# Attention, gated layer and routed experts on one core: other places for the first loads, and another first expert step

## The chip, the cores and the metric

The program runs on one core of a Trainium2 chip. The metric is the time of one execution on the device in microseconds (us). TensorE (PE) multiplies, VectorE (DVE), ScalarE (ACT) and GpSimd (POOL) work element by element, and SyncE (SP) issues most transfers. A lower time is better.

## The reference

Three stages follow each other. All inputs are 32-bit floats.

```
# attention: 4 batches x 8 heads, 576 positions, 64 wide
scores = q @ k.T / 8 + (cum[:, None] - cum[None, :])   # cum = cumsum(log(clip(f, 1e-4, 1)))
scores = where(above the diagonal, -1e9, scores)
attn   = exp(scores - rowmax) ;  attn /= attn.sum + 1e-9 ;  x = attn @ v
# gated layer: 2304 tokens x 512, 1536 inside
x = (sigmoid(x @ w_gate) * (x @ w_val)) @ w_out
# routing to 8 experts with 288 places each: the largest logits x @ w_gate2 choose first
order = argsort(-logits.flatten())
for idx in order: give the token to the expert, if the token is free and the expert has a place
# experts, 1024 inside
out[tokens of e] = maximum(x[tokens of e] @ w1[e], 0) @ w2[e]
```

## The kernel before, in words

The order of the work is written out by hand: each engine runs its instructions in the order in which the code names them, and waits only for data and for free buffers. Transfers that SyncE issues go through one queue.

**Attention** (`attention`) goes head by head. For a pair of heads `load` brings q and k, transposed, into one of three buffers (`raw`), and `load_v` the values (`vf`). `prep` copies a head on ScalarE into `P` (`P1`, one of four buffers) in the reduced 32-bit float of TensorE, `prep2` computes the rests that this copy loses on GpSimd into `p` (`P2`), and `copies` fills the other half of `p` from `P` by two transfers. The decay enters as two rows of `P`: heads 0 and 1 get them from `ck` (`decay`), all others get them with the load, from a copy of all decay rows in device memory (`ckd`), which `decays` reads back (`raw<-ckd`) and which therefore must have landed. `ones` and the memsets in the list of `P1` set the rows of ones that belong to them.

Then `maxpass` computes the scores roughly and takes each row's maximum on VectorE, `mrows` turns the maxima into a row (`mr`), and `mstore` sends this row of 2.5 KB into row 66 of `P` (`P<-mr`). Only with it in place can `scores` run: it subtracts the maximum inside the matmul (`py`, `p1b`). ScalarE takes the exponentials (`e`), GpSimd cuts the diagonal blocks, and `av` multiplies by the values one head later. In the steady state of the loop, head h runs `scores(h)`, then `av(h-1)` with the row of maxima of head h+2 and the maxima of head h+3 between its matmuls. Heads 0 to 2 have an order of their own. `warm` gives TensorE matmuls without use while nothing else is there. From head 2 on `fill` loads the first weights of the gated layer (`mr<-ww`, two transfers of 512 KB at head 2).

**Into the first expert.** After the gated layer and the routing (`Route`), the tokens of the first expert are gathered by their indices (`First.gather`, three gathers of 96 rows on GpSimd), and one late tile of tokens is multiplied by a 0/1 matrix `hot` instead. `First.turn` turns them: for each quarter of the 512 values three matmuls by the identity and one by `hot`, then ScalarE and VectorE split the result into `xe0h` and `xe0l`. `filler` gives TensorE the last matmuls of the gated layer meanwhile. `Experts.split` splits a block of expert weights (`eraw`, or `fraw` for the first four) into `ehi` on ScalarE and `elo` on GpSimd, every fourth block after the first on VectorE. `experts` then runs per expert layer 1 (`eh`, `hh`, `hl`) and layer 2 (`ey`).

Of the kernel before, what the change touches and what calls it, by code (L numbers as in the profile page):

```python
# [34 lines left out]
def make_consts(ev, pool, keep):  # L35

    nc = ev.nc

    jp = pool.tile([128, 128], I32, name="jp")
    nc.gpsimd.iota(jp, pattern=[[1, 128]], base=0, channel_multiplier=-1)  # L40
    ev.identb = pool.tile([128, 128], BF16, name="identb")
    nc.vector.tensor_scalar(ev.identb, jp, 0.0, None, op0=OP.is_equal)
    yield
    ev.mq = pool.tile([128, S], BF16, name="mq")
    nc.vector.memset(ev.mq[:, :448], 0.0)
    nc.vector.tensor_scalar(ev.mq[:, 448:], jp, 0.0, BIG, op0=OP.is_gt, op1=OP.mult)
    ev.identr = pool.tile([128, 128], F32R, name="identr")
    nc.vector.tensor_scalar(ev.identr, jp, 0.0, None, op0=OP.is_equal)
    yield
    ev.ident = keep.tile([128, 128], F32, name="ident")  # L50
    nc.vector.tensor_scalar(ev.ident, jp, 0.0, None, op0=OP.is_equal)
    yield

AT = (2, 4)
FIRST = {2: -3, 4: -2, 5: -1}
WARM = (19, 4, 6, 2)
KT = [(0, 0, 0, 1024), (0, 128, 128, 0), (0, 256, 256, 512), (0, 384, 384, 832), (64, 448, 512, 448)]


def attention(ev, qkT, vr, f, xs, rec, ckd, fill):
# [4 lines left out]
    with ExitStack() as ctx:  # L67
# [11 lines left out]
        def load(p):  # L79
            r = RAW3[p % 3]  # L80
            nc.sync.dma_start(r[0:64], qkT[2 * p:2 * p + 2].rearrange("h d s -> d h s"))
            RAW[2 * p], RAW[2 * p + 1] = r[:, 0], r[:, 1]
# [7 lines left out]
            nc.sync.dma_start(VF[p], vr[p])  # L90

        load(0)
        load(1)
        consts = make_consts(ev, st, ev.consts)
        zero = st.tile([NHEAD, 1], F32, name="zero")
        idle = st.tile([NHEAD, 1], F32, name="warm")
# [1 line left out]
        nc.scalar.activation(idle, zero, AF.Ln, bias=1.0)  # L98
        next(consts)
        P1 = [st.tile([67, 64 + 2 * S], F32R, name=f"P1_{i}") for i in range(4)]  # L100
        for t in P1:
            nc.gpsimd.memset(t[64:67].bitcast(F32), 1.0)
            nc.gpsimd.memset(t[0:64, 0:64].bitcast(F32), 0.0)

        junk = st.tile([128, 1600], BF16, name="mj")
        JT = (0, 64, 256, 576, 1024)
        ck = st.tile([NHEAD, 2, S], F32R, name="ck")
        next(consts)
        nc.vector.tensor_scalar(ft, ft, 1e-4, 1.0, op0=OP.max, op1=OP.min)
        nc.scalar.activation(ft, ft, AF.Ln)  # L110
        cum = st.tile([NHEAD, S], F32, name="cum")
        nc.vector.tensor_tensor_scan(cum, ft, zero.to_broadcast([NHEAD, S]), 0.0, op0=OP.add, op1=OP.add)
        nc.vector.tensor_scalar(ck[:, 0], cum, -8.0, None, op0=OP.mult)
        nc.vector.scalar_tensor_tensor(ck[:, 1], cum, -8.0, ck[:, 0], op0=OP.mult, op1=OP.subtract)

        def ones(p):
            nc.gpsimd.memset(RAW3[p][64:66, :, :S], 1.0)
# [9 lines left out]
        def decay(h):  # L127
            nc.sync.dma_start(P1[h % 4][64:66, K0:].bitcast(F32), ck[h:h + 1].bitcast(F32))
# [46 lines left out]
        def maxpass(h):  # L175
            for _ in maxparts(h):
                pass
# [7 lines left out]
        def mstore(h):  # L185
            nc.sync.dma_start(P1[h % 4][66:67, 0:640].bitcast(F32), MR.pop(h))
# [73 lines left out]
        warm(WARM[0])  # L260
        for h in (0, 1):
            decay(h)
        nc.sync.dma_start(ckd.rearrange("r h s -> h r s"), ck.bitcast(F32))
        for h in (0, 1):
            prep(h, 64)
# [21 lines left out]
        load_v(0)  # L287
        copies(2)
        decays(2)
        load(2)  # L290
        copies(3)
        warm(WARM[3])
        maxpass(2)
# [1 line left out]
        ones(2)  # L295
        for h in range(1, NHEAD):
            odd = h % 2
            scores(h, 3 if h == 2 else None)
            if h == 1:
                ones(0)  # L300
            if h == 2:
                mstore(3)
                next(consts)

            def rows(r):
                if r < NHEAD:
                    mrows(r)
                    mstore(r)

            def early():  # L310
                rows(h + 2 if h > 1 else 2)
                if h == 1:
                    prep(4)
                    prep2(4)
                elif h + 4 < NHEAD:
                    prep(h + 4)

            def late():
                if h + 3 < NHEAD:
                    maxpass(h + 3)  # L320

            if h == 1:
                av(0, {2: early, 3: lambda: maxpass(3)})
                prep(5)
            elif h == 2:
                av(1, {0: lambda: maxpass(4), 5: early})
                late()
            else:
                av(h - 1, {AT[0]: early, AT[1]: late})
            if h < NHEAD - 3:  # L330
                copies(h + 3)
            if h >= 3 and odd:
                store(h // 2 - 1)
            if h == 1:
                load(3)
                decays(3)
            if not odd and h // 2 + 3 < NPAIR:
                load(h // 2 + 3)
                decays(h // 2 + 3)
            if odd and h // 2 + 1 < NPAIR:  # L340
                load_v(h // 2 + 1)
            for b in range(B - 1):
                step = {2: 0, 4: 1, 5: 2}.get(h - (b + 1) * H)
                if step is not None:
                    recip(b, step)
            if h + 4 < NHEAD:
                prep2(h + 4)
            if h in FIRST:
                fill(FIRST[h])
            fill(h)  # L350
# [596 lines left out]
class Experts:  # L947
# [24 lines left out]
    def split(self, n, part=None, after=None):  # L972

        if part is not None:
            nc, c = self.ev.nc, slice(512 * part, 512 * part + 512)
            if part == 0:
                self.hi[n] = self.first.tile([128, 1024], F32R, name=f"ehi{n % 12}", bufs=1)
                self.lo[n] = self.first.tile([128, 1024], F32R, name=f"elo{n % 12}", bufs=1)
                nc.scalar.activation(self.hi[n], self.raw[n], AF.Copy)
            nc.gpsimd.tensor_copy(self.gate, after)  # L980
            nc.gpsimd.tensor_tensor(self.lo[n][:, c], self.raw[n][:, c], self.hi[n][:, c], op=OP.subtract)
            if part:
                del self.raw[n]
                if n < 3:
                    self.load(n + 1)
        elif n < 8 * E:
            nc, r = self.ev.nc, self.raw.pop(n)
            pool = self.first if n % 12 < 4 else self.pool
            hi = self.hi[n] = pool.tile([128, 1024], F32R, name=f"ehi{n % 12}", bufs=1)
            lo = self.lo[n] = pool.tile([128, 1024], F32R, name=f"elo{n % 12}", bufs=1)  # L990
            nc.scalar.activation(hi, r, AF.Copy)  # L991
            eng = nc.vector if n % 4 == 3 and n > 3 else nc.gpsimd
            eng.tensor_tensor(lo, r, hi, op=OP.subtract)  # L993
            self.load(n + RAWS)

# [5 lines left out]
class First:  # L1001
# [7 lines left out]
        self.xg = [t[:TT] for t in (slots[:, :DM], slots[:, DM:], big)]  # L1009
        self.x = [pool.tile([128, 4, CH], F32R, name=n) for n in ("xe0h", "xe0l")]  # L1010

    def gather(self, route):
        nc = self.nc
        for i in range(3):
            nc.gpsimd.indirect_dma_start(out=self.xg[i], out_offset=None, in_=self.x2d,  # L1015
                                         in_offset=bass.IndirectOffsetOnAxis(ap=self.ev.idx[:, i:i + 1], axis=0))
        places = self.places[:, :CH].bitcast(I32)
        nc.gpsimd.iota(places, pattern=[[1, CH]], base=0, channel_multiplier=0)
        nc.vector.tensor_scalar(self.hot[:, :CH], places, route.slot[:, LAST:LAST + 1], None, op0=OP.is_equal)  # L1019

    def turn(self, x, bank):

        nc = self.nc
        for k in range(4):
            ks = slice(k * 128, (k + 1) * 128)
            p = bank()
            for i in range(3):
                nc.tensor.matmul(p[:, i * TT:(i + 1) * TT], self.xg[i][:, ks], self.ev.ident[:TT, :TT], start=i == 0,  # L1028
                                 stop=False, skip_group_check=True)
            nc.tensor.matmul(p[:, :CH], x[:, ks], self.hot[:, :CH], start=False, stop=True, skip_group_check=True)  # L1030
            nc.scalar.activation(self.x[0][:, k], p[:, :CH], AF.Copy)
            nc.vector.tensor_tensor(self.x[1][:, k], p[:, :CH], self.x[0][:, k], op=OP.subtract)


def experts(ev, W, x2d, first, idx, out, wk, psum):
# [108 lines left out]
def network(tc, qk, vv, f, ww, bcT, w1, w2, cb, cf, out):  # L1144
# [3 lines left out]
    with ExitStack() as ctx:  # L1148
# [86 lines left out]
            R.round(r == 0, FILL[5] if r < ROUNDS - 1 else 6, lambda: r and EW.split((r - 1) // 2, (r - 1) % 2, R.c[:1, 0, :1, 0]))  # L1235
        a = R.settle()
        R.permutation(a)
        filler(left - 2 * 3 * NF)
        X0 = First(ev, ep, scratch, x2d)
        X0.gather(R)  # L1240
        for part in range(2):
            EW.split(3, part, ev.idx[:1, :1])
        filler(left)
        next(rest, 0)
        X0.turn(xd, F.bank)
# [2 lines left out]
        ps.close()  # L1248
        EW.pool = pool("ew")
        xw = pool("xw", bufs=2)  # L1250
        pools = {n: pool("xp_" + n, bufs=b, space=PSUM) for n, b in (("h", 3), ("y", 2), ("t", 3))}
        experts(ev, EW, x2d, X0.x, ev.idx, out, xw, lambda n: pools[n].tile([128, 512], F32, name="e" + n))


# [28 lines left out]
```

## Time and profile before

| | |
|---|---|
| median of 3 runs | 921.29 us (920.33 to 921.76) |
| the profiled execution | 920.34 us, span 918.4 us |
| TensorE busy | 899.2 us (98%) |
| VectorE, ScalarE, GpSimd busy | 549.5, 330.2, 461.4 us |
| moved by transfers | 111.30 MB, mean 121 GB/s |

Times in the profile count from the span's start. A busy TensorE is not a fast one: the granted clock says how much of its full speed it had. An engine's idle time is put down to what ended last before the waiting instruction started.

### The profile page before, as it was taken

How to read it: one execution, taken by the hardware profiler on the slowest of the kernel's cores; microseconds unless marked ns; L12 is line 12 of the kernel's file. 1: busy time of each engine (PE TensorE's matmuls, PEld its weight loads, DVE VectorE, ACT ScalarE, POOL GpSimd, SP SyncE). 2: the span in 40 equal slices, each digit the busy share in tenths (PEclk: the TensorE clock that was granted, in tenths of full speed). 3: DMA queues.
4: the chain of work that ended last, by engine and by line, in shares of the span. 5: the costliest groups of instructions: out<-in, count | busy, mean ns of one | idle time of the engine just before them, and what ended most of it. 6: DMA issues, size and time to landing. Idle time of an engine off the chain costs nothing. (4 is left out here: it accounts for less than half of the span.)

```text
span 918.4 us, 14090 instructions
## 1 busy us (share of the span) xinstructions
PE 899.2 (98%) x5206; PEld 753.1 (82%) x5206; DVE 549.5 (60%) x1183; ACT 330.2 (36%) x570; POOL 461.4 (50%) x393
## 2 busy tenths in 40 slices
PE   8899999999999999999999999999999999999995
PEld 5677777778788888888888887887788999999995
DVE  5387887918885497988989642525523443444431
ACT  5566677642323111121111221221125444444530
POOL 8678899825555122121222221321158777777741
PEclk9899999999999999999999999999999999999998
DMA  6788899745652203010121210011257666657610
GB/s 141 169 209 224 228 233 251 205 121 184 164 163 64 75 1 92 18 67 9 46 63 26 67 46 1 1 44 46 71 166 228 195 189 194 199 169 210 206 32 26
DMA packets 49016, 111.30 MB, mean 121 GB/s; under 512 B 11346, under 2 KB 11762, under 8 KB 48946
## 3 DMA queue, kind: packets, MB, share of 16 engines
q1 hardware_dynamic: 44786, 98.85, 38.6%
q0 software_dynamic: 3072, 9.44, 3.2%
q10 hardware_dynamic: 1088, 2.10, 0.7%
q8 instruction: 41, 0.67, 0.3%
q14 instruction: 29, 0.24, 0.1%
HBM read 86.12 MB, written 14.71 MB: 110 GB/s over the span
## 5 line engine op out<-in xcount | busy, mean ns | idle before, releaser
L509 POOL TENSOR_TENSOR gl<-sg,gh 128x512 fp32r<-128x512 f32 x36 | 49.5, 1375 | 201.0 <-ACT gh L508 201.0
L993 POOL TENSOR_TENSOR elo<-eraw,ehi 128x1024 fp32r<-128x1024 f32 x45 | 109.0, 2431 | 43.0 <-ACT ehi L991 42.6
L141 PE MATMUL pv<-e,vf 128*65 128x256 f32 (+1 forms) x434 | 106.6, 370 | 0.0
L500 PE MATMUL gv<-xah,w_hi 128*128 128x512 f32 (+1 forms) x288 | 103.1, 358 | 0.0
L500 PE MATMUL gv<-xah,w_lo 128*128 128x512 f32 (+1 forms) x288 | 102.7, 357 | 0.0
L500 PE MATMUL gv<-xal,w_hi 128*128 128x512 f32 (+1 forms) x288 | 102.7, 357 | 0.0
L542 DVE CUSTOM_DVE_ANT_0 mb<-mb,bc 128x512 f32<-128x512 f32 x96 | 82.1, 856 | 3.3
L542 DVE CUSTOM_DVE_ANT_0 mb<-mr,bc 128x512 f32<-128x512 f32 x96 | 81.7, 851 | 2.8
L508 ACT ACTIVATE gh<-sg 128x512 fp32r<-128x512 f32 x36 | 22.8, 633 | 156.4 <-PE o L521 84.2
L1080 PE MATMUL ey<-hh,ehi 128*128 128x288 f32 x256 | 78.2, 305 | 0.0
L500 PE MATMUL gv<-xbh,w_hi 128*128 128x512 f32 x192 | 76.7, 399 | 0.0
L1080 PE MATMUL ey<-hl,ehi 128*128 128x288 f32 x256 | 76.3, 298 | 0.0
L1080 PE MATMUL ey<-hh,elo 128*128 128x288 f32 x256 | 75.9, 296 | 0.0
L500 PE MATMUL gv<-xbh,w_lo 128*128 128x512 f32 x192 | 75.9, 395 | 0.0
L500 PE MATMUL gv<-xbl,w_hi 128*128 128x512 f32 x192 | 75.8, 395 | 0.0
L141 PEld LDWEIGHTS pv<-e,vf 128*65 128x65 f32 x434 | 50.4, 139 | 24.1 <-issue 15.4
L1067 PE MATMUL eh<-xeh,ehi 128*128 128x288 f32 x224 | 68.0, 304 | 0.0
L1070 DVE SCALAR_TENSOR_TENSOR hl<-eh,hh 128x288 fp32r<-128x288 f32 x64 | 29.0, 456 | 63.8 <-ACT hh L1069 63.8
L157 DVE CUSTOM_DVE_ANT_0 mj<-p1b,mq 128x192 bf16<-128x192 f32 (+3 forms) x128 | 46.6, 418 | 34.3 <-PE p1b L141 34.2
L141 PE MATMUL p1b<-P 66*128 66x192 f32 (+7 forms) x256 | 65.9, 326 | 0.9 <-DVE mx L157 0.4
L1067 PE MATMUL eh<-xeh,elo 128*128 128x288 f32 x224 | 66.4, 297 | 0.0
L1067 PE MATMUL eh<-xel,ehi 128*128 128x288 f32 x224 | 66.4, 296 | 0.0
(214 smaller groups left out, 2304.8 us busy)
## 6 DMA issues: line engine op xcount, KB each, us to landing
eraw<-w SPq DMA_DIRECT2D x56, 512.0 KB
mr<-ww SPq DMA_DIRECT2D x26, 512.0 KB
raw<-qk SPq DMA_DIRECT2D x16, 576.0 KB
p<-P SPq DMA_DIRECT2D x64, 144.0 KB
vf<-vv SPq DMA_DIRECT2D x16, 330.0 KB
bc<-ww SPq DMA_DIRECT2D x10, 512.0 KB
xs<-xo SPq DMA_DIRECT2D x16, 292.5 KB
x2d<-mr SPq DMA_DIRECT2D x17, 256.0 KB
```

What stands on the lines that cost most here:

```text
L141: nc.tensor.matmul(out, lhsT, rhs, start=start, stop=stop, skip_group_check=True)
L157: nc.vector.tensor_tensor_reduce(out=junk[:, JT[t]:JT[t] + n], in0=src, in1=ev.mq[:, S - n:], op0=OP.add, op1=OP.min, scale=-1.0, scalar=3 ...
L500: nc.tensor.matmul(p[i][:, :m], w_[:, ws], x_[:, k], start=n == 0, stop=n == 11)
L508: nc.scalar.activation(hi, s, AF.Copy)
L509: nc.gpsimd.tensor_tensor(lo, s, hi, op=OP.subtract)
L542: nc.vector.tensor_tensor_reduce(out=junk, in0=a, in1=self.bc[j], op0=OP.mult, op1=OP.add, scale=1.0, scalar=0.0, accum_out=res)
L993: eng.tensor_tensor(lo, r, hi, op=OP.subtract)
L1067: nc.tensor.matmul(p[:, :CH], w_[:, ws], x_[:, k], start=n == 0, stop=n == 11)
L1070: nc.vector.scalar_tensor_tensor(h[1][:, f], p[:, :CH], 0.0, h[0][:, f], op0=OP.max, op1=OP.subtract)
L1080: nc.tensor.matmul(p[:, :CH], w_[:, ws], h_[:, f], start=n == 0, stop=n == 23)
```

## The change

In the first heads the loads of q and k, the rows of maxima and the copies of heads 4 and 5 change places on SyncE's queue, and the work of heads 1 to 3 is ordered anew around them. The fixed rows of `P1` are set by ScalarE and VectorE. In the step into the first expert, `hot` and the last halves of `elo` come before the gathers, the turns by the identity become transposes that all come before the products by `hot`, block 7 of the expert weights is split on GpSimd, and the PSUM pools are laid out in another order. The identity matrix is made later.

```
@@ attention @@
-WARM = (19, 4, 6, 2)
+WARM = (18, 4, 6, 2)
         load(0)
-        load(1)
...
-        for t in P1:
-            nc.gpsimd.memset(t[64:67].bitcast(F32), 1.0)
-            nc.gpsimd.memset(t[0:64, 0:64].bitcast(F32), 0.0)
...
         nc.scalar.activation(ft, ft, AF.Ln)
+        for t in P1[:2]:
+            nc.scalar.activation(t[64:67], zero[0:3].to_broadcast([3, 64 + 2 * S]), AF.Copy, bias=1.0)
...
+        for t in P1[2:]:
+            nc.vector.memset(t[64:67].bitcast(F32), 1.0)
...
         for h in (0, 1):
             decay(h)
+        load(1)
+        for t in P1:
+            nc.gpsimd.memset(t[0:64, 0:64].bitcast(F32), 0.0)
         nc.sync.dma_start(ckd.rearrange("r h s -> h r s"), ck.bitcast(F32))
...
         decays(2)
-        load(2)
         copies(3)
...
-            scores(h, 3 if h == 2 else None)
-            if h == 1:
-                ones(0)
             if h == 2:
+                mrows(3)
                 mstore(3)
-                next(consts)
+                load(3)
+                decays(3)
+                load_v(1)
+            scores(h)
...
             if h == 1:
-                av(0, {2: early, 3: lambda: maxpass(3)})
+                ones(0)
+                av(0, {2: lambda: rows(2), 3: lambda: maxpass(3)})
+                load(2)
+            elif h == 2:
+                prep(4)
+                prep2(4)
+                av(1)
                 prep(5)
-            elif h == 2:
-                av(1, {0: lambda: maxpass(4), 5: early})
+                prep2(5)
+                maxpass(4)
+            elif h == 3:
+                av(2, {2: lambda: rows(4), 3: lambda: maxpass(5), 5: lambda: prep(6)})
+                rows(5)
+                prep(7)
                 late()
+                prep2(6)
...
-            if h < NHEAD - 3:
+            if h == 2:
+                copies(4)
+                copies(5)
+            elif 2 < h < NHEAD - 3:
                 copies(h + 3)
...
-            if h == 1:
-                load(3)
-                decays(3)
+            if h == 2:
+                load_v(2)
...
-            if odd and h // 2 + 1 < NPAIR:
-                load_v(h // 2 + 1)
+            if odd and h > 1 and h // 2 + 2 < NPAIR:
+                load_v(h // 2 + 2)
...
+            if h > NHEAD - 3:
+                next(consts)
@@ Experts.split @@
-            eng = nc.vector if n % 4 == 3 and n > 3 else nc.gpsimd
+            eng = nc.vector if n % 4 == 3 and n > 7 else nc.gpsimd
@@ First @@
+    def tokens(self, route):
+        places = self.places[:, :CH].bitcast(I32)
+        nc.gpsimd.iota(places, ...)
+        nc.vector.tensor_scalar(self.hot[:, :CH], places, route.slot[:, LAST:LAST + 1], None, op0=OP.is_equal)
...
     def turn(self, x, bank):
+        for i in range(3):
+            for k in range(4):
+                nc.tensor.matmul(p[k][:, i * TT:(i + 1) * TT], self.xg[i][:, rows[k]], self.ev.ident[:TT, :TT], start=i == 0,
+                                 stop=False, is_transpose=True, skip_group_check=True)
         for k in range(4):
-            for i in range(3):
-                nc.tensor.matmul(p[:, i * TT:(i + 1) * TT], self.xg[i][:, ks], self.ev.ident[:TT, :TT], start=i == 0,
-                                 stop=False, skip_group_check=True)
...
@@ network @@
+        X0 = First(ev, ep, scratch, x2d)
+        X0.tokens(R)
+        for part in range(2):
+            EW.split(3, part, X0.hot[:1, :1])
         filler(left - 2 * 3 * NF)
-        X0.gather(R)
-        for part in range(2):
-            EW.split(3, part, ev.idx[:1, :1])
+        X0.gather()
         filler(left)
...
-        ... (("h", 3), ("y", 2), ("t", 3))}
+        ... (("t", 3), ("y", 2), ("h", 3))}
```

SyncE's queue at the program's start, before; `raw_103` takes heads 0 and 1, `raw_104` heads 2 and 3, `P_0` and `P_1` are the buffers of heads 0 and 1:

```order
L81 DMA raw_103<-qk 64x2x1152
L81 DMA raw_104<-qk 64x2x1152
L128 DMA P_0_116<-ck 2x1x576
L128 DMA P_1_117<-ck 2x1x576
L263 DMA ckd<-ck 32x2x576
L132 DMA p_165<-P_0_116 64x576
L133 DMA p_165<-P_0_116 64x576
L86 DMA raw_104<-ckd 2x2x576
L132 DMA p_167<-P_1_117 64x576
L133 DMA p_167<-P_1_117 64x576
L186 DMA P_0_116<-mr 1x5x128
```

The same place now:

```order
L82 DMA raw_103<-qk 64x2x1152
L128 DMA P_0_115<-ck 2x1x576
L128 DMA P_1_116<-ck 2x1x576
L82 DMA raw_104<-qk 64x2x1152
L266 DMA ckd<-ck 32x2x576
L132 DMA p_164<-P_0_115 64x576
L133 DMA p_164<-P_0_115 64x576
L87 DMA raw_104<-ckd 2x2x576
L132 DMA p_166<-P_1_116 64x576
L133 DMA p_166<-P_1_116 64x576
L186 DMA P_0_115<-mr 1x5x128
```

The second load of q and k has moved behind the two decay rows and stands directly ahead of the store of `ckd`.

SyncE's queue at heads 2 and 3, before, from the values of heads 2 and 3 on; `P_3`, `P_0` and `P_1` are here the buffers of heads 3, 4 and 5, `raw_104` takes heads 8 and 9, and `mr_428` and `mr_430` are the first weights of the gated layer:

```order
L90 DMA vf<-vv 128x660
L186 DMA P_3_119<-mr 1x5x128
L186 DMA P_0_116<-mr 1x5x128
L132 DMA p_341<-P_1_117 64x576
L133 DMA p_341<-P_1_117 64x576
L81 DMA raw_104<-qk 64x2x1152
L86 DMA raw_104<-ckd 2x2x576
L396 DMA mr_428<-ww 128x512
L396 DMA mr_430<-ww 128x512
L186 DMA P_1_117<-mr 1x5x128
```

The same transfers now, from the values of heads 2 and 3 on:

```order
L91 DMA vf<-vv 128x660
L132 DMA p_365<-P_0_115 64x576
L133 DMA p_365<-P_0_115 64x576
L132 DMA p_378<-P_1_116 64x576
L133 DMA p_378<-P_1_116 64x576
L91 DMA vf<-vv 128x660
L82 DMA raw_104<-qk 64x2x1152
L87 DMA raw_104<-ckd 2x2x576
L411 DMA mr_404<-ww 128x512
L411 DMA mr_406<-ww 128x512
L186 DMA P_0_115<-mr 1x5x128
L186 DMA P_1_116<-mr 1x5x128
```

The row of maxima of head 4 (`P_0<-mr`) has moved from ahead of the load and the two weight transfers to behind them; the load of heads 4 and 5 and that of heads 6 and 7, not in these rows, now stand behind the rows of heads 2 and 3.

GpSimd at the step into the first expert, before; `x2d` holds the tokens, `elo` the rests of the weights:

```order
L1015 DMA mr_5435<-x2d,idx 96x512 x2
L1015 DMA mr_5434<-x2d,idx 96x512
L1018 IOTA mb_5436 128x288
L980 CAST gate<-idx 1x1
L981 TENSOR_TENSOR elo_6132<-fraw,ehi_6131 128x512
L980 CAST gate<-idx 1x1
L981 TENSOR_TENSOR elo_6132<-fraw,ehi_6131 128x512
L1045 DMA xg<-x2d,idx 96x512 x3
```

The same place now:

```order
L1031 IOTA mb_5435 128x288
L995 COPY gate<-mb_5436 1x1
L996 TENSOR_TENSOR elo_6128<-fraw,ehi_6127 128x512
L995 COPY gate<-mb_5436 1x1
L996 TENSOR_TENSOR elo_6128<-fraw,ehi_6127 128x512
L1037 DMA mr_5434<-x2d,idx 96x512 x2
L1037 DMA mr_5433<-x2d,idx 96x512
L1065 DMA xg<-x2d,idx 96x512 x3
```

The three gathers have moved behind the two halves of `elo`, which now wait for `hot` (`mb_5436`) instead of the indices.

## Rows read from the trace of the kernel before

**Rows 1.** Page, busy times; then stretches: us, busy (instructions), clock, transfers.

```profile
PE 899.2 (98%) x5206; PEld 753.1 (82%) x5206; DVE 549.5 (60%) x1183; ACT 330.2 (36%) x570; POOL 461.4 (50%) x393
...
680.00:700.00 20.00, 16.96 (x115) 16.58 (x115) 7.46 (x11) 10.58 (x17) 14.56 (x8) 0.91 0.85 263
```

**Rows 2.** Who waited for whom, TensorE: us in total, times, longest.

```profile
PE eh L1067 <- DVE hl L1070: 2.1, 1, 2.1
PE py L141 <- DMA P<-mr: 2.0, 1, 2.0
PE eh L1067 <- DVE xe0l L1032: 1.0, 1, 1.0
...
PE p1b L141 <- ACT e L206: 0.4, 1, 0.4
```

**Rows 3.** SyncE in order of time, first heads: start, us to issue, transfer.

```profile
9.33 0.39 SPq L263 DMA_DIRECT2D ckd<-ck  x1
...
11.50 0.24 SPq L86 DMA_DIRECT2D raw<-ckd  x1
...
13.12 2.96 SPq L186 DMA_DIRECT2D P<-mr  x2
...
18.32 0.67 SPq L81 DMA_DIRECT2D raw<-qk  x1
...
21.62 0.75 SPq L186 DMA_DIRECT2D P<-mr  x1
```

**Rows 4.** TensorE in order of time: scores of heads 0, 2, 4; layer 1's first.

```profile
15.01 0.39 PE L141 MATMUL py<-P 67*128 67x256 f32 x1
...
26.11 0.38 PE L141 MATMUL py<-P 67*128 67x256 f32 x1 [2.04 <-DMA P<-mr]
...
42.13 0.52 PE L141 MATMUL py<-P 67*128 67x256 f32 x1
...
681.12 0.40 PE L1067 MATMUL eh<-xe0h,ehi 128*128 128x288 f32 x1 [0.99 <-DVE xe0l L1032]
```

**Rows 5.** Stretches: PE, PEld, DVE, ACT, POOL busy, clock, transfer share, GB/s.

```profile
37.00:53.00 16.00, 16.00 (x98) 12.31 (x97) 10.04 (x36) 10.28 (x17) 11.36 (x13) 1.00 0.90 237
27.00:33.50 6.50, 6.14 (x23) 4.16 (x22) 2.21 (x10) 2.04 (x5) 5.40 (x6) 0.65 0.87 190
...
28.90:35.70 6.80, 6.80 (x21) 4.16 (x20) 2.21 (x10) 1.20 (x4) 3.63 (x4) 0.50 0.55 127
...
694.55:697.95 3.40, 3.32 (x14) 3.31 (x15) 0.75 (x3) 1.09 (x2) 3.40 (x2) 0.50 0.91 293
```

**Rows 6.** Page, transfers: destination<-source, count, size of one.

```profile
mr<-ww SPq DMA_DIRECT2D x26, 512.0 KB
raw<-qk SPq DMA_DIRECT2D x16, 576.0 KB
p<-P SPq DMA_DIRECT2D x64, 144.0 KB
vf<-vv SPq DMA_DIRECT2D x16, 330.0 KB
```

**Rows 7.** Chain that ended last: start, us, turns, a product by hot, later transposes.

```profile
676.66 0.64 PE gv L1028 x6
677.30 0.52 PE gv L1030 x2
...
701.46 0.25 PE et L1055 x3
```

**Rows 8.** GpSimd, TensorE's weight loads and ScalarE in order of time.

```profile
671.59 0.92 POOL L1015 DMA_INDIRECT mr<-x2d,idx  x1 [0.30 <-issue]
...
672.99 1.28 POOL L981 TENSOR_TENSOR elo<-fraw,ehi 128x512 fp32r<-128x512 f32 x1
...
675.17 0.30 PEld L1028 LDWEIGHTS gv<-ident,mr 96*128 96x128 f32 x2 [0.26 <-DMA mr<-x2d,idx]
...
687.22 1.06 ACT L991 ACTIVATE ehi<-eraw 128x1024 fp32r<-128x1024 f32 x1 [1.67 <-DMA eraw<-w]
```

More of the change, by code (lines that the diff above doesn't have):

```diff
@@ L52, in make_consts @@
     yield
+    yield
 AT = (2, 4)
 FIRST = {2: -3, 4: -2, 5: -1}
-WARM = (19, 4, 6, 2)
+WARM = (18, 4, 6, 2)
 KT = [(0, 0, 0, 1024), (0, 128, 128, 0), (0, 256, 256, 512), (0, 384, 384, 832), (64, 448, 512, 448)]
@@ L310, in early @@
             def early():
-                rows(h + 2 if h > 1 else 2)
-                if h == 1:
-                    prep(4)
-                    prep2(4)
-                elif h + 4 < NHEAD:
+                rows(h + 2)
+                if h + 4 < NHEAD:
                     prep(h + 4)
@@ L333, in attention @@
                 store(h // 2 - 1)
-            if h == 1:
-                load(3)
-                decays(3)
+            if h == 2:
+                load_v(2)
             if not odd and h // 2 + 3 < NPAIR:
@@ L345, in attention @@
                     recip(b, step)
-            if h + 4 < NHEAD:
+            if 2 < h < NHEAD - 4:
                 prep2(h + 4)
+            if h > NHEAD - 3:
+                next(consts)
             if h in FIRST:
@@ L1010, in __init__, with gather @@
         self.x = [pool.tile([128, 4, CH], F32R, name=n) for n in ("xe0h", "xe0l")]
-    def gather(self, route):
+    def tokens(self, route):
+        nc = self.nc
+        places = self.places[:, :CH].bitcast(I32)
+        nc.gpsimd.iota(places, pattern=[[1, CH]], base=0, channel_multiplier=0)
+        nc.vector.tensor_scalar(self.hot[:, :CH], places, route.slot[:, LAST:LAST + 1], None, op0=OP.is_equal)
+    def gather(self):
         nc = self.nc
@@ L1016, in gather @@
                                          in_offset=bass.IndirectOffsetOnAxis(ap=self.ev.idx[:, i:i + 1], axis=0))
-        places = self.places[:, :CH].bitcast(I32)
-        nc.gpsimd.iota(places, pattern=[[1, CH]], base=0, channel_multiplier=0)
-        nc.vector.tensor_scalar(self.hot[:, :CH], places, route.slot[:, LAST:LAST + 1], None, op0=OP.is_equal)
     def turn(self, x, bank):
         nc = self.nc
-        for k in range(4):
-            ks = slice(k * 128, (k + 1) * 128)
-            p = bank()
-            for i in range(3):
-                nc.tensor.matmul(p[:, i * TT:(i + 1) * TT], self.xg[i][:, ks], self.ev.ident[:TT, :TT], start=i == 0,
-                                 stop=False, skip_group_check=True)
-            nc.tensor.matmul(p[:, :CH], x[:, ks], self.hot[:, :CH], start=False, stop=True, skip_group_check=True)
-            nc.scalar.activation(self.x[0][:, k], p[:, :CH], AF.Copy)
-            nc.vector.tensor_tensor(self.x[1][:, k], p[:, :CH], self.x[0][:, k], op=OP.subtract)
+        p = [bank() for _ in range(4)]
+        rows = [slice(k * 128, (k + 1) * 128) for k in range(4)]
+        for i in range(3):
+            for k in range(4):
+                nc.tensor.matmul(p[k][:, i * TT:(i + 1) * TT], self.xg[i][:, rows[k]], self.ev.ident[:TT, :TT], start=i == 0,
+                                 stop=False, is_transpose=True, skip_group_check=True)
+        for k in range(4):
+            nc.tensor.matmul(p[k][:, :CH], x[:, rows[k]], self.hot[:, :CH], start=False, stop=True, skip_group_check=True)
+            nc.scalar.activation(self.x[0][:, k], p[k][:, :CH], AF.Copy)
+            nc.vector.tensor_tensor(self.x[1][:, k], p[k][:, :CH], self.x[0][:, k], op=OP.subtract)
 def experts(ev, W, x2d, first, idx, out, wk, psum):
@@ L1237, in network @@
         R.permutation(a)
+        X0 = First(ev, ep, scratch, x2d)
+        X0.tokens(R)
+        for part in range(2):
+            EW.split(3, part, X0.hot[:1, :1])
         filler(left - 2 * 3 * NF)
-        X0 = First(ev, ep, scratch, x2d)
-        X0.gather(R)
-        for part in range(2):
-            EW.split(3, part, ev.idx[:1, :1])
+        X0.gather()
         filler(left)
@@ L1250, in network @@
         xw = pool("xw", bufs=2)
-        pools = {n: pool("xp_" + n, bufs=b, space=PSUM) for n, b in (("h", 3), ("y", 2), ("t", 3))}
+        pools = {n: pool("xp_" + n, bufs=b, space=PSUM) for n, b in (("t", 3), ("y", 2), ("h", 3))}
         experts(ev, EW, x2d, X0.x, ev.idx, out, xw, lambda n: pools[n].tile([128, 512], F32, name="e" + n))
```

## The prediction

> **What bounds the kernel now.** I read the busy shares first, then the stretches, then the chain of waits and the list of who waited for whom. TensorE is busy for 98% of the span, so the change can only win where TensorE stands still or runs slowly, and it can lose wherever it makes it wait [rows 1]. The stretches show two such places in the stages that the change touches: the step into the first expert, where TensorE is busy for 16.96 of 20 us at a granted clock of 0.91 [rows 1], and the first heads, where the clock is 0.50 for 6.8 us [rows 5]. The waits give them names: 2.0 us in the first heads for the row of maxima of head 2 (P<-mr) and 0.4 us for an exponential, and at the experts 1.0 us for the last xe0l and 2.1 us for an hl [rows 2].
>
> How the first wait comes about is to be seen on SyncE's queue and on TensorE [rows 3, 4]. The row of head 0 is issued at 13.12 and TensorE goes on with it at 15.01, 1.9 us later. The row of head 2 is issued at 21.62 and TensorE can use it only at 26.11, 4.5 us later. It has the same 2.5 KB. What differs is what was issued just ahead of it: a load of 576 KB at 18.32, with copies behind it. So a small transfer on this queue lands behind the bytes ahead of it. The rate at which such a mix drains is 190 GB/s in one full stretch and 237 GB/s in another [rows 5].
>
> After each of the two long waits TensorE ran at 0.50, that is at 1.2 GHz instead of 2.4: 28.90 to 35.70, and 694.55 to 697.95 [rows 5]. Half of each is lost: 3.4 and 1.7 us. Heads of full speed follow the first from 36 us on; the scores of head 4 start at 42.13 [rows 4]. From there to the end of attention TensorE has no wait of note, so a shift of that start is a shift of the end.
>
> **What goes in the first heads.** The load of heads 4 and 5 now stands behind the row of head 2. That takes away the wait of 2.0, the 0.4 behind an exponential (the maxima of head 4 are now computed after it) and the slow clock of 3.4: minus 5.8 us.
>
> **What comes, at head 0.** The load of heads 2 and 3 used to be issued right behind the first one. It now stands behind the two decay rows and ahead of the store of ckd, and the load of the ckd rows (raw<-ckd) waits for that store to land. Queued behind that waiting load on SyncE are the two copies of head 1 and then the row of head 0. Before, ckd was issued at 9.33, its reader at 11.50, the row at 13.12 [rows 3]. Now 576 KB, 0.59 MB [rows 6], drain first: 2.5 us at 237 GB/s, 3.1 at 190. Everything behind ckd's landing moves by as much, the row too, and the scores of head 0 start at about 18.0 instead of 15.01. TensorE has nothing but finished warm-up work there. I take plus 3.0, since a lone load is nearest to the lower rate; the bounds are 0.7 (the store passes the load, and only the load's own issue time of 0.67 is in the way) and 3.7 (both). Moving the ones of P1 from GpSimd to ScalarE and VectorE and dropping one warm-up matmul I cost at nothing: that work ends before the row does. Without this cover it would be some tenths of a microsecond either way.
>
> The Trainium skill ("DMA: Bandwidth & Descriptors", section "Queues, rings and completion order") says that each DMA engine takes the descriptors of a queue in ring order, but that completion is not first in, first out over a queue, so that a later small transfer on few engines can be done before an earlier one on all sixteen. By its first half the row waits as in the last paragraph, by its second it need not; the 4.5 us of head 2 side with the first half, and the second is the first rival below.
>
> **What comes, at head 4.** In before the row of head 4 was issued one head ahead of the load of heads 8 and 9 and of the two weight loads; now it stands behind them. And the queue never runs dry on the way there. The row of head 2 is issued at 21.62 plus 3.0, that is 24.6, and the next load 0.75 later at 25.4. From there to the row of head 4 stand three raw loads of 576 KB, two vf of 330, four copies of 144 and two weight loads of 512 [rows 6]: 3988 KB, 4.08 MB, which is 17.2 us at 237 GB/s and 21.5 at 190. With the 1.9 us of an unhindered row it lands at 44.5 to 48.8. TensorE, without the waits taken away, is ready for the scores of head 4 at 42.13 minus 5.8 plus 3.0, or 39.3. A wait of 5.2 to 9.5 us; I take 5.5, because the 237 are of a stretch with the same kinds (weights, loads, copies, vf) and the 190 of one with a load and little else. Its lower bound is nothing, if the row passes what is ahead. If the clock is low before, row and readiness both move and this term stays.
>
> **The clock behind both.** Two waits of 2.0 us each brought a slow stretch that cost 1.7 and 3.4 us [rows 2, 5]. The two new waits are longer, so I set 2.6 for each, 5.2 together, between 3.4 and 6.8; the lower bound is nothing.
>
> **The first expert.** Four edits. (a) The 12 turns by the identity become transposes. Three of the old ones take 0.64 us, three transposes with the same operands' size at L1055 take 0.25 [rows 7], and all of them can run before the four matmuls by hot, 0.52 each. (b) hot is made earlier, but the two halves of elo, 1.28 each, now run on GpSimd ahead of the three gathers. The third gather ended its issue at 671.59 plus 0.92, and TensorE saw it land at 675.17 [rows 8]. It can move by nothing, if the halves are done before the stores that are gathered land, or by 2.6, both halves; I take 1.6, so 676.8. Then four transposes (0.33) and four products (2.1): layer 1 starts at 679.2. (c) PSUM pools in another order: the first layer-1 matmul needs only the first quarter of x, so the 1.0 us for xe0l is gone. Layer 1 starts at 681.12 in before [rows 4], so minus 1.9, between minus 3.5 and minus 0.6. Of this 1.1 is taken back (0 to 1.9): ScalarE's second ehi waited for its weights until 687.22 [rows 8], and it issues these behind its last quarter of x, which comes earlier by less than layer 1 does. (d) The elo of the fourth weight block goes from VectorE to GpSimd. On VectorE it stood ahead of the hl that held TensorE for 2.1; on GpSimd it is late only if layer 2 asks for it sooner than it is done. That takes 2.1 away and the slow clock of 1.7. In all 1.9 minus 1.1 plus 2.1 plus 1.7: minus 4.6 us; bounds minus 7.3, and nothing (late gathers and a late elo eat all of it).
>
> **Other edits**, at nothing: ident is made at head 30, long before its first use; load_v comes earlier into a third buffer whose readers are done; both lie beside full TensorE work.
>
> **The sum.** Minus 5.8, plus 3.0, plus 5.5, plus 5.2, minus 4.6: plus 3.3 us. The profiled run of before took 920.34 (span 918.4), the median of the runs is 921.29, 0.95 above it. On the first scale that gives 923.6, on the second 924.6; I forecast 924.5.
>
> **Rivals.** First, on the other side: the small row is not held by what is ahead of it, and head 2's wait had a reason of its own. Then the 5.5 at head 4 and its clock go; the 3.0 at head 0 stay, since there SyncE itself waits for ckd. Minus 5.8, plus 3.0, plus 2.6, minus 4.6: minus 4.8, 916.5 us on the scale of the median. It decides as soon as the row of head 4 lands less than about 4 us behind its issue. For it speaks that the row has only 2.5 KB; against it the 4.5 us of head 2. Chance 0.15.
>
> Second: waits as forecast, but no slow stretch behind them. Plus 3.3 minus 5.2: minus 1.9, 919.4 us. Against it: both waits of before had one. For it: they differed twofold in length, so the clock is not a fixed price. Chance 0.17.
>
> Third: the step into the expert gives only 1 of its 4.6 us, with GpSimd late for gathers or for the extra elo: plus 6.9, 928.2 us. For it: GpSimd is the busiest of the other engines there, with 14.56 of 20 us [rows 1], and two jobs more stand in its queue. Against it: the gathers had less than 0.3 us of wait behind them [rows 8], and the work added ahead of them is small beside their landing. Chance 0.13.
>
> The forecast keeps 0.55, with a range of its own from 921.5 to 928. A measurement of this kernel tells about 0.2% from no change, 1.84 us: below 919.4 is faster, above 923.1 slower. Faster gets the first rival and half of the second, 0.24; the same gets the other half and a tenth from the forecast's lower edge, 0.18; slower the rest, 0.58. The range from 917.5 to 930 leaves out most of the first rival below and the third with slow clocks above.
>
> **What would show it.** In the trace of the changed kernel: py of head 0 waits about 3 us for P<-mr and starts near 18; py of head 2 does not wait; py of head 4 waits 4 us or more for P<-mr and starts at 45 to 50; a granted clock of 0.50 behind both. At the expert: the first eh starts 1 to 3 us earlier against its neighbours and waits for no xe0l, nothing in layer 1 waits for hl, and the clock stays at 1.00. I am wrong if py of head 4 waits under 2 us, if the clock holds, or if layer 1 of the first expert stalls.

## The result, and the profile after

The changed kernel takes 927.63 us (median of 5 runs, 925.43 to 928.14), the kernel before 920.50 (5 runs); the ratio is 1.0073, 95% interval 1.0053 to 1.0093. It is slower, as forecast, inside the range of 917.5 to 930, and 3.1 us above the forecast of 924.5. The profiled execution took 926.05 us with a span of 924.0, 5.6 us more than the span before; the terms below are told on that scale. The 1.5 us by which the median of the runs moved more are not in this trace.

The waits of TensorE now, in the form of [rows 2] (us in total, times, longest):

```profile
PE py L141 <- DMA P<-mr: 7.5, 2, 3.8
...
PE pv L141 <- DMA vf<-vv: 0.8, 1, 0.8
...
PE gv L1047 <- DMA mr<-x2d,idx: 0.7, 1, 0.7
...
PE eh L1087 <- DVE hl L1090: 0.6, 2, 0.3
```

The one long wait for a row of maxima has become two, and the waits for xe0l and the long one for hl are gone. TensorE in order of time has, against [rows 4], the scores of heads 0, 2, 4 and 5, the gated layer's first matmul and layer 1's first:

```profile
17.65 0.39 PE L141 MATMUL py<-P 67*128 67x256 f32 x1 [3.74 <-DMA P<-mr]
...
31.12 0.33 PE L141 MATMUL py<-P 67*128 67x256 f32 x1
...
49.17 0.42 PE L141 MATMUL py<-P 67*128 67x256 f32 x1 [3.76 <-DMA P<-mr]
...
57.82 0.52 PE L141 MATMUL py<-P 67*128 67x256 f32 x1
...
209.94 0.64 PE L515 MATMUL gv<-xah,w_hi 128*128 128x512 f32 x1
...
689.19 0.51 PE L1087 MATMUL eh<-xe0h,ehi 128*128 128x288 f32 x1
```

One more row of the kernel before is needed beside it, the same first matmul of the gated layer there:

```profile
199.05 0.64 PE L500 MATMUL gv<-xah,w_hi 128*128 128x512 f32 x1
```

So attention ends 10.9 us later (209.94 against 199.05). From there to layer 1 it is 479.25 us instead of 482.07, 2.8 less, and from layer 1 to the end of the span 234.8 instead of 237.3, 2.5 less. 10.9 minus 2.8 minus 2.5 is the 5.6.

SyncE's queue in order of time shows both new waits at their source; it answers to [rows 3]:

```profile
8.10 0.67 SPq L82 DMA_DIRECT2D raw<-qk  x1
8.81 0.59 SPq L266 DMA_DIRECT2D ckd<-ck  x1
...
14.13 0.24 SPq L87 DMA_DIRECT2D raw<-ckd  x1
...
15.66 2.14 SPq L186 DMA_DIRECT2D P<-mr  x2
...
28.14 0.74 SPq L186 DMA_DIRECT2D P<-mr  x1
...
39.62 0.65 SPq L82 DMA_DIRECT2D raw<-qk  x1
...
40.80 0.81 SPq L411 DMA_DIRECT2D mr<-ww  x2
41.71 3.86 SPq L186 DMA_DIRECT2D P<-mr  x2
```

The store of ckd is issued 0.5 us sooner than before, but its reader 2.6 later: 5.3 us lie between the two issues where it was 2.2. The row of head 0 follows at 15.66. The row of head 4 is issued at 41.71 and TensorE goes on at 49.17, 7.5 us later. The row of head 2, with nothing big ahead of it, is issued at 28.14, and TensorE starts these scores at 31.12 without a wait.

Behind both waits TensorE ran slowly. The stretches, with the columns of [rows 5]:

```profile
18.90:29.10 10.20, 10.20 (x39) 8.54 (x38) 2.54 (x13) 4.60 (x8) 7.77 (x9) 0.51 0.33 91
49.60:56.40 6.80, 6.80 (x23) 5.13 (x23) 0.00 (x0) 3.18 (x5) 1.34 (x3) 0.51 0.20 67
```

10.2 and 6.8 us at 1.2 GHz, half of each lost: 8.5 us together, where the prediction had 5.2.

### The profile page after: what moved, and what is told of

It is laid out like the page before. It is cut to its first block, busy times and chain, and to the rows that moved or that the text cites. A ratio compares the mean times of both kernels' runs of the same rounds, so it can differ in the third digit from the quotient of the medians.

```text
span 924.0 us, 14086 instructions
## 1 busy us (share of the span) xinstructions
PE 899.7 (97%) x5193; PEld 752.9 (81%) x5193; DVE 544.3 (59%) x1184; ACT 333.3 (36%) x572; POOL 458.2 (50%) x390
## 5 line engine op out<-in xcount | busy, mean ns | idle before, releaser
L141 PE MATMUL p1b<-P 66*128 66x192 f32 (+7 forms) x256 | 68.2, 335 | 2.4 <-DMA P<-ck 1.3
L1006 ACT ACTIVATE ehi<-eraw 128x1024 fp32r<-128x1024 f32 x60 | 63.3, 1056 | 9.9 <-DMA eraw<-w 9.8
```

The costliest lines, as they stand in the source:

```text
L141: nc.tensor.matmul(out, lhsT, rhs, start=start, stop=stop, skip_group_check=True)
```

## The experiments

Each was timed against the kernel before on the same chip, but not all on one chip, so the rows of the table are compared with each other by their ratios. Single executions of one kernel lie up to 6 us from its median, so a verdict rests on the ratio and its interval, and a place on the trace. The last column is read from the one profiled execution of each kernel.

| edit | median us | ratio to before | gated layer starts at us |
|---|---|---|---|
| the whole change | 927.63 | 1.0073 (1.0053 to 1.0093) | 209.9 |
| attention part alone | 932.09 | 1.0105 (1.0088 to 1.0122) | 212.0 |
| expert part alone | 918.18 | 0.9969 (0.9955 to 0.9984) | 203.2 |
| block 7 on GpSimd alone | 917.76 | 0.9975 (0.9953 to 0.9996) | 198.9 |
| load of heads 2, 3 back at the start | 919.67 | 0.9984 (0.9969 to 1.0000) | 206.8 |
| row of head 4 ahead of load and weights | 922.92 | 1.0010 (0.9993 to 1.0027) | 204.7 |
| both | 916.68 | 0.9954 (0.9935 to 0.9972) | 198.6 |
| warm matmuls in the waits | 919.36 | 0.9992 (0.9976 to 1.0008) | 200.9 |
| row of head 4 in ScalarE's queue | 926.83 | 1.0074 (1.0046 to 1.0102) | 209.2 |
| rows of heads 2 and 4 there | 922.69 (1 run) | | 206.8 |
| start as before, weights behind the rows | 912.92 | 0.9901 (0.9871 to 0.9930) | 201.5 |
| start as before, load between the rows | 912.61 | 0.9900 (0.9866 to 0.9934) | 198.0 |
| the same with 7 warm matmuls | 912.53 | 0.9906 (0.9887 to 0.9925) | 194.5 |

### The two parts by themselves

The first kernel has the changed attention and the old expert step, the second the other way round:

```
attention() of the changed kernel,  Experts.split, First, network as before
attention() as before,              Experts.split, First, network of the changed kernel
```

> 

> The attention part of the change alone, with the old expert step. Theory (two independent parts): the gated layer's first matmul comes 10.9 us later, as in the changed kernel, and nothing after it changes, so 920.5 plus 10.9, about 931.4 us. Rival (the expert step's gain hangs on the later start, or is none): the same 927.6 as the whole change.

> 

> The expert part of the change alone, on the old attention. Theory: attention ends as before, layer 1 of the first expert starts 2.8 us earlier and the wait of 2.05 for hl and its slow clock are gone, less what the weights take back: minus 5.3, about 915.2 us. Rival (earlier layer 1 only runs into late weights): minus 2 or less, 918.5 or above.

The attention part alone costs 1.05% (9.7 us, 8.1 to 11.2 by the interval), where 10.9 were expected, with the waits of the whole change. Its trace ends attention 2.1 us later than that of the whole change, with a wait of 1.33 us for VectorE's maxima at 177.31 and a slow stretch behind it. The expert part alone gives 0.31% (2.9 us, 1.5 to 4.1 by the interval), less than the 5.3 expected: the median lies between theory and rival, nearer to the rival's 918.5. In its trace the stages themselves gave what they gave in the whole change: 479.42 us from the gated layer to layer 1 and 235.1 from there to the end, 4.8 less than before together. But in this execution attention, whose code is that of before, ended 4.1 us later, at 203.2. Some 3.3 of them are a wait for VectorE's maxima late in attention and a clock of 0.57 for 4 us behind it:

```profile
168.38 0.47 PE L141 MATMUL p1b<-P 67*128 67x448 f32 x1 [1.94 <-DVE mx L157]
```

The kernel before waited 0.40 us there in its profiled execution. Such a wait for the maxima of a late head is in some of the traces and not in others, from none to 1.9 us, also between kernels with the same attention; what decides it is open.

### Block 7 on GpSimd alone

```
-            eng = nc.vector if n % 4 == 3 and n > 3 else nc.gpsimd
+            eng = nc.vector if n % 4 == 3 and n > 7 else nc.gpsimd
```

> 

> The kernel before with one edit: block 7 of the expert weights is split on GpSimd instead of VectorE. Theory: the wait of 2.05 us for hl at 694.6 and the slow clock behind it (1.7) go, and nothing new comes: minus 3.7, about 916.8 us. Rival (on GpSimd the elo is late for layer 2, which then waits for it): minus 1 or less, 919.5 or above.

From layer 1's first matmul to the end of the span it is 3.9 us less than before (233.4 against 237.3), no wait for hl is left and none for elo came; the medians give 0.25% (0.4 to 4.3 us). The theory held. In the whole change this edit is the same, yet the stage behind layer 1's start gained only 2.5: 1.4 us were given back. The two waits of 0.2 and 0.3 us for hl shown above are 0.6 of that; that the rest also comes of the earlier start, as the prediction argued, is likely but not shown.

### The load of heads 2 and 3 back at the start

```
         load(0)
+        load(1)
...
         for h in (0, 1):
             decay(h)
-        load(1)
```

> 

> The whole change, but with the load of heads 2 and 3 back at the program's start. Theory (the store of ckd drains behind this load, and the slow clock behind head 0 comes from the wait): the reader of ckd is issued near 11.5 again, py of head 0 starts near 15.0 without a wait of note, and the clock of 0.50 from 18.8 to 28.1 is gone: minus 2.6 minus 4.6, about 920.4 us; the wait at head 4 stays near 3.8. Rival A (the slow clock has another cause than the wait): minus 2.6, 925.0 us. Rival B (the row of head 0 is late for the new places of the ones): py of head 0 stays near 17.6, no change, 927.6.

The scores of head 0 are back at 15.00 and run on at full clock. The time fell to 919.67, near the theory's 920.4. One thing it had not: at head 4 TensorE now came sooner and waited 4.9 us instead of 3.8. Below are its scores of heads 0 and 4, SyncE's issue of the rows of heads 4 and 5, and the slow stretch, which here began while TensorE still waited:

```profile
15.00 0.39 PE L142 MATMUL py<-P 67*128 67x256 f32 x1
...
43.29 0.58 PE L142 MATMUL py<-P 67*128 67x256 f32 x1 [4.93 <-DMA P<-mr]
```

```profile
35.85 2.66 SPq L187 DMA_DIRECT2D P<-mr  x2
```

```profile
40.80:51.00 10.20, 7.71 (x26) 6.03 (x27) 0.27 (x1) 3.17 (x5) 3.19 (x5) 0.51 0.39 121
```

From the issue of the row of head 4 to its use it is 7.4 us, as in the whole change.

### The row of head 4 ahead of the load and the weights

```
-FIRST = {2: -3, 4: -2, 5: -1}
+FIRST = {4: -2, 5: -1}
...
                 rows(5)
+                load(4)
+                decays(4)
+                fill(-3)
...
-            if not odd and h // 2 + 3 < NPAIR:
+            if not odd and h > 2 and h // 2 + 3 < NPAIR:
```

> 

> The whole change, but the load of heads 8 and 9, its decay rows and the first two weight loads are issued behind the rows of heads 4 and 5. Theory (the row of head 4 drains behind those 1600 KB): the row is usable 2 to 3 us after its issue, py of head 4 waits under 1 us, the slow clock behind it is gone: minus 3.4 minus 3.4, about 921 us. Rival A (the bytes ahead of those, copies, vf and the load of heads 6 and 7, hold it as well): minus 2 or less, 925.5 or above. Rival B (the later load makes head 8 wait instead): the gain at head 4 stands in the trace, but a new wait near 65 us takes 2 us or more of it.

The wait for the row of head 4 is gone, with its slow clock. Smaller waits stand in its place: the one for the values of heads 2 and 3, 0.85 us in the whole change, is 1.56 here, although nothing ahead of their load was moved, and one for the row of head 6 is new:

```profile
40.30 1.16 PE L141 MATMUL pv<-e,vf 128*65 128x256 f32 x4 [1.56 <-DMA vf<-vv]
45.63 0.28 PE L141 MATMUL py<-P 67*128 67x256 f32 x1
50.97 0.52 PE L141 MATMUL py<-P 67*128 67x256 f32 x1
...
58.41 0.39 PE L141 MATMUL py<-P 67*128 67x256 f32 x1 [0.52 <-DMA P<-mr]
```

So what was issued ahead of the row held it, and the row of head 6, which now stands behind the moved transfers, waits a little in its turn. By the ratios the kernel gained 0.6%, some 5.8 us, and attention ends 5.3 us sooner in the trace; the theory had 6.8, and the difference is within the noise.

### Both edits together

> 

> The whole change with both edits: the load of heads 2 and 3 back at the start, and the load of heads 8 and 9 and the first weights behind the rows of heads 4 and 5. Theory (two independent waits, each with its slow clock): minus 7.3 and minus 6.8, 927.6 to about 913.5 us, 7 us under the kernel before. Rival (once TensorE is early at head 0, the transfers are what it waits for at heads 2 to 4 anyway): 917 us or above, with a wait for a row or a load in the first eight heads.

916.68, so the rival was nearer than the theory. Attention ends at 198.6, no sooner than in the kernel before (199.05); what is left of the gain is the expert part. No slow clock is in these heads, but the DMA engines stood still for 5 us while the load stood behind two rows:

```profile
35.00:40.00 5.00, 4.73 (x30) 3.47 (x28) 3.85 (x19) 3.31 (x6) 4.15 (x6) 1.00 0.02 7
```

TensorE then waited 0.8 us for the row of head 6; 1.6 us for the values of heads 2 and 3 it had lost at 33.79, ahead of the pause.

### Work without use in the two waits

```
         mstore(1)
+        warm(16)
         scores(0)
...
+            if h == 4:
+                warm(16)
             scores(h)
```

> 

> The whole change, with 16 matmuls without use (some 3.4 us at full speed) ahead of the scores of head 0 and 16 ahead of those of head 4, in the time in which TensorE waits for the rows. They change no transfer. Theory (the slow clock comes of the idle wait, and costs 4.6 and 3.4 us): py of heads 0 and 4 start within 0.5 us of where they do now relative to their rows, the clock stays at 1.00 behind both, minus 8, about 919.6 us. Rival A (the slow clock comes of the mix of work behind the waits): no gain, 927 to 928. Rival B (it comes of idle time, but the time saved is lost again to later waits for transfers): the clock stays at 1.00, but waits of some us appear behind, and under 4 us are saved.

No transfer was changed. The row of head 4 is still used only 7.1 us after its issue (37.56 and 44.65). The granted clock is 1.00 all through both places, and 8.3 us of the median are gone (927.63 to 919.36), or 0.8% by the ratios; the theory had 8.0:

```profile
18.00:29.00 11.00, 11.00 (x69) 8.70 (x68) 4.29 (x20) 7.14 (x13) 8.49 (x10) 1.00 0.56 136
44.00:56.00 12.00, 11.36 (x69) 8.77 (x69) 7.03 (x22) 6.65 (x11) 6.88 (x8) 1.00 0.53 139
```

With the clock kept up the changed kernel is as fast as the kernel before (0.9992, 0.9976 to 1.0008): the loss of the change is as large as the cost of the slow clock behind its two waits. Idle time brought that on, not the mix of work behind the waits, which is the same here.

### The row in a queue of its own

```
-            nc.sync.dma_start(P1[...], MR.pop(h))
+            q = nc.scalar if h == 4 else nc.sync      # second kernel: h in (2, 4)
+            q.dma_start(P1[...], MR.pop(h))
```

> 

> The whole change, with the row of head 4 alone issued by ScalarE into its own queue instead of SyncE's; the loads stay where they are. Theory A (the row waits for its turn behind the bytes ahead of it in SyncE's queue): in a queue of its own it lands about 2 us after its issue, py of head 4 starts by 44.5 to 46, minus 3.4 minus 3.4, about 921 us. Rival B (the sixteen engines themselves are full, whatever the queue): py of head 4 still waits 2 us or more, 925 us or above.

> 

> The whole change with the rows of heads 2 and 4 both issued by ScalarE into its own queue. It tells whether that queue is slow by itself. Theory (bytes ahead in the engines, not the queue, hold a row): the row of head 2, issued when almost nothing else is under way (2 GB/s ahead of it), is usable 1.5 to 3 us after its issue, and py of head 2 waits under 1 us; the row of head 4 again takes 5 to 7 us. Rival (ScalarE's queue is slow by itself): the row of head 2 takes 5 us or more too, and py of head 2 waits 2 us or more.

The first kernel's row of head 4 was still late:

```profile
41.50 1.28 ACTq L187 DMA_DIRECT2D P<-mr  x1
...
48.02 0.39 PE L141 MATMUL py<-P 67*128 67x256 f32 x1 [2.62 <-DMA P<-mr]
```

6.5 us from issue to use, against 7.5 in SyncE's queue, and no gain in time. The second kernel has the rows of heads 2 and 4 in that queue:

```profile
28.82 1.29 ACTq L187 DMA_DIRECT2D P<-mr  x1
31.28 0.33 PE L141 MATMUL py<-P 67*128 67x256 f32 x1
...
41.79 0.69 ACTq L187 DMA_DIRECT2D P<-mr  x1
48.39 0.39 PE L141 MATMUL py<-P 67*128 67x256 f32 x1 [2.66 <-DMA P<-mr]
```

The row of head 2, with the DMA engines' busy share at 0.02 behind its issue, was used 2.5 us after it, without a wait, the row of head 4 after 6.6. The queue is not slow by itself; what is already under way in the DMA engines, which were busy throughout from 41.5 to 48.0 in the first kernel, holds a small row, in either queue. The Trainium skill ("DMA: Bandwidth & Descriptors", section "Issuing engines are not separate DMA queues") says that transfers started by any engine run on the same 16 DMA engines and interleave, and that starting them elsewhere saves only issue time. This trace agrees in that another queue gave the row little, 6.5 against 7.5 us.

### Two versions with fewer bytes ahead of the row

Both have the load of heads 2 and 3 at the start. The first moves only the two weight transfers behind the rows of heads 4 and 5. The second puts the load of heads 8 and 9 between these two rows, and the values of heads 2 and 3 right behind the load of heads 4 and 5:

```
 first:          rows(5)
+                fill(-3)
 second:
-                ... {2: lambda: rows(4), ...
+                ... {2: lambda: (rows(4), load(4), decays(4)), ...
                 rows(5)
+                fill(-3)
...
                 load(2)
+                load_v(1)
```

> 

> The load of heads 2 and 3 back at the start, as in load1_first, and only the two weight loads (1.05 MB of the bytes ahead of the row of head 4) moved behind the rows of heads 4 and 5; the load of heads 8 and 9 stays ahead. Theory (the row's wait is the bytes ahead of it): the row lands 2.6 to 4.4 us sooner (1.05 MB at 400 to 237 GB/s) than in load1_first, where py of head 4 waited 4.9 us; the wait shrinks to 0.5 to 2.3 and no slow clock follows: minus 3 to minus 4 and minus 3.4, 912.5 to 913.5 us. Rival (the load of q and k holds it, however few bytes follow): py of head 4 waits 3.5 us or more with a slow clock behind, 918 or above.

> 

> As both_first, but the load of heads 8 and 9 stands between the rows of heads 4 and 5, and the values of heads 2 and 3 are loaded right behind q and k of heads 4 and 5. In both_first the DMA engines stood still from 35 to 40 us (share 0.02), and TensorE then waited 1.6 us for vf, 0.9 ahead of av of head 5 and 0.8 for the row of head 6. Theory (those waits come of the bytes that piled up behind the pause): they go, and the gated layer starts 2 to 4 us sooner than at 198.6: 912.5 to 914.5 us. Rival (the transfers of the first eight heads fill the engines whatever their order): new waits of the same sum appear later, and the time stays within 1.5 us of 916.7.

Both are 1.0% faster than the kernel before, with medians in the expected ranges. The first differs from both edits together only in the place of the load of heads 8 and 9, and it is 0.5% faster (0.9901 against 0.9954); its DMA engines paused there for under 2 us instead of 5. In the first the wait at head 4 fell from 4.9 to 0.27 us; SyncE's issue of the row and TensorE's use of it:

```profile
37.58 4.03 SPq L187 DMA_DIRECT2D P<-mr  x2
```

```profile
41.75 0.39 PE L142 MATMUL py<-P 67*128 67x256 f32 x1 [0.27 <-DMA P<-mr]
```

With 1.05 MB fewer ahead of it the row is used 4.2 us after its issue instead of 7.4, 3.3 sooner, where 2.6 to 4.4 were expected, although the load of heads 8 and 9 still stands there: the rival is ruled out, and the number of bytes decides. The rest of the fall is TensorE's own: in this execution it ran slowly from 11.6 to 18.4 us and came to head 4 some 3 us later, while the row was issued 1.7 later. The trace of the second has no wait for a row, nor for the values. Its DMA engines still paused, but from 36 to 39 us only. What is left is a wait at the maxima of head 4 and a slow stretch behind it, so that the gated layer starts only 0.6 us sooner than with both edits (197.99 against 198.59), where 2 to 4 were expected:

```profile
30.22 0.76 PE L142 MATMUL p1b<-P 66*128 66x192 f32 x4 [1.42 <-ACT P L125]
...
41.34 0.28 PE L142 MATMUL py<-P 67*128 67x256 f32 x1
46.67 0.52 PE L142 MATMUL py<-P 67*128 67x256 f32 x1
```

### Work without use in that wait

```
+                warm(7, "py")
                 maxpass(4)
```

The `"py"` names the buffers in which these matmuls write.

> 

> As load4_between, with 7 matmuls without use (some 1.5 us) ahead of the maxima of head 4, where TensorE there waited 1.4 us for the copy P of head 4 and then ran at 0.50 from about 31 to 38 us. Nothing else changes. Theory (the idle wait brings the slow clock): the maxima of head 4 start where they did, the clock stays at 1.00 and the gated layer starts some 3 us sooner than at 198.0: 909 to 910 us, ratio to before 0.985 to 0.988. Rival (TensorE then only meets the transfers earlier): the clock stays at 1.00, but waits of 2 us or more come at heads 4 to 8, and the ratio stays near 0.990.

In the trace it did what the theory says. The wait and the slow clock are gone, heads 4 to 8 have no wait for a transfer, and the gated layer starts 3.5 us sooner:

```profile
194.47 0.64 PE L517 MATMUL gv<-xah,w_hi 128*128 128x512 f32 x1
```

The span is 908.5 us. But the median of 912.53 and the ratio of 0.9906 are those of the version without the edit, and the ratio is the rival's, without the waits that the rival foresaw. The profiled executions were 914.66 us there, above its median, and 910.53 here, below its own; whether most executions of the version without the edit had that slow stretch is not known. So this last edit is not shown to gain anything.

## Why the prediction was right, and where it was off

**What goes in the first heads** (minus 5.8): right. Head 2 waits for no row, no exponential holds TensorE there, and the stretch at 0.50 from 28.90 to 35.70 is at full clock from 29.10 on.

**Head 0** (plus 3.0): right, 2.6 measured (17.65 against 15.01). The path was the one told: load, store of ckd, its reader, copies, row. Moving the load back gave 15.00.

**Head 4** (plus 5.5): right in its mechanism, and in size partly by luck. The row landed 20.2 us after the issue of the load behind the row of head 2 (28.93 to 49.17), where the prediction had 19.1 to 23.4, although the queue did run low on the way (a busy share of 0.37 from 33 to 34 us). But the row's wait was only 3.8 us, under the 5.2 to 9.5 that had been worked out. The values of heads 2 and 3, whose place the prediction had at nothing, held TensorE for 0.85 more, and waits of 0.2 and 0.3 for ScalarE make it 5.1. TensorE came to head 4 later than the 39.3 of the prediction, since its slow clock after head 0 had cost it 5.1; the prediction said that the row would then move with it and the term stay, but the row moved less, and without that slow clock, with the load of heads 2 and 3 back at the start, the wait was 4.9. Its scores started at 49.17, inside the 45 to 50.

**The reason given for it** was too narrow in one word. The row lands behind the bytes ahead of it, but not because they are ahead of it on this queue: in a queue of its own it was nearly as late. The first rival, that the row passes, is ruled out twice, by 7.5 us here and by 6.5 in the other queue.

**The clock behind both waits** (plus 5.2): the term that was mis-sized. It was set at 2.6 for each wait, the mean of the two stretches of before, between 3.4 and 6.8 in all; the stretches were 10.2 and 6.8 us long and cost 8.5, 3.3 more than forecast and above the upper bound. The prediction's reason for a larger term, that the new waits are longer, is not borne out: waits of nearly the same length had stretches of 10.2 and 6.8 us behind them, and the wait of 2.0 before had one of 6.8 too. The second rival (no slow clock) is ruled out by the trace, and by the warm matmuls, which kept the clock up and gave back 8.3 us of the median.

**The first expert** (minus 4.6): minus 5.3 in the trace. Layer 1 starts 2.8 sooner, not 1.9; the edit on block 7 is worth 3.9 by itself, as told (2.1 and 1.7); and 1.4 was taken back, where 1.1 was forecast. The clock stays at 1.00, as told, but the sign that nothing in layer 1 waits for hl failed by two short waits, 0.6 us together. GpSimd is late only by the 0.7 us for which the turns wait for the last gathers, so the third rival did not come about. In the medians the part alone gave 2.9, between 1.5 and 4.1, so its size is less sure than the trace makes it.

**The sum.** 3.3, plus 3.3 for the clock, minus 0.4 at head 0, minus 0.4 at head 4, minus 0.7 at the experts, and 0.4 for a wait for VectorE's maxima in a later head (0.84 us at 131.95 in this execution, 0.40 at 165.91 in that of before) gives 5.5 of the 5.6 us.

## What to carry to other kernels

Ask of every moved transfer which small one is issued behind it, and count the bytes in flight rather than the place in the queue: here 1.05 MB fewer ahead of a row of 2.5 KB brought it into use 3.3 us sooner, and another queue 0.9 us. A wait of TensorE can have a second price behind it that is larger than the first; ask for the slow stretch in the trace and, where the wait can't go, try work without use in it. An edit that lets one engine arrive sooner is worth only what the transfers can follow, so keep the DMA engines from pausing as well: both edits together gained 0.5%, and 1.0% with one load put back ahead of the rows.

## What the runs showed of the hardware

The length of a slow stretch did not go with the length of the wait in a simple way. Waits of 3.74 and 3.76 us were followed by 10.2 and 6.8 us at 0.50, one of 4.93 by a stretch of 10.2 that began within it, one of 1.42 by 6.8 us:

```profile
31.10:37.90 6.80, 6.80 (x26) 5.62 (x26) 2.08 (x11) 3.62 (x6) 5.74 (x6) 0.52 0.61 145
```

and one of 1.56 us, in the kernel with the row of head 4 ahead, by none. What decides that is open. A transfer issued by ScalarE held that engine for 0.69 to 1.29 us, which its own queue of work has to bear.
